# Two groups instead of four for the routing of blocks 6 to 11, with marks made on VectorE, low parts of the first weight pieces on GpSimd, and block 10's row turn inside block 11

## Chip, cores and metric

One core of a Trainium2 chip runs the whole program in one launch. The metric is device time in microseconds. The kernel before ran three times, and the median counts; one more execution was profiled.

## The reference

A linear attention with decay, and behind it a mixture of experts in which each token goes to one expert. What matters of it:

```python
state = gamma * state + einsum('bhd,bhe->bhde', k_t, v_t)      # for each of 768 steps, 4 batches, 8 heads
y_t = scale * einsum('bhd,bhde->bhe', q_t, state)              # head_dim 64
x = y as 3072 rows of 512
xn, en = x / (norm(x) + 1e-6), expert_emb / (norm(expert_emb) + 1e-6)
logits = xn @ en.T / tau                                        # 8 experts
expert_idx, gate = argmax(logits), softmax(logits) at expert_idx
for e in range(8):
    h = relu(x[expert_idx == e] @ w1[e])                        # 512 x 1024
    out[expert_idx == e] = gate * (h @ w2[e])                   # 1024 x 512
```

All in fp32.

## The kernel before, in words

**Blocks.** The 3072 tokens are worked off in 12 blocks of 256 (`for m in range(NM)`, m is 0 to 11). Each block computes scores (L388) that VectorE masks (L408) into `pm`, the part of y from the state (`inter`) and from the block itself (`intra`, both L451), and the state of the next block (L422). TensorE also transposes the next block's keys and queries (L357, L375) in four sets of four. ScalarE copies results out of PSUM (`take`, L467 and L470; L362, L376). VectorE turns the rows of y (L475, `rows_turn`) and SyncE writes them to a table of rows `xd` in HBM (L485, `rows`).

**Banks.** Transpositions, scores, logits and the routing's small products share four PSUM banks in turn (`pt_`, names `b`). A product that takes a bank waits until the bank's reader is done.

**Routing.** Blocks are routed in groups (`GROUPS`). For a group: logits of each block (L498, transposed by VectorE at L506 into `parts`), `sums` (L516), `choose` and `add_counts` (VectorE), `count` (L543 to L547), `ranks`, `split_ranks` (VectorE), `mark`, and `table`. `mark` makes, for each half block of 128 tokens, a 128x128 tile that holds the token's number where its rank stands and 0 elsewhere; ScalarE makes it with two operations (L601, L602). `table` multiplies these by VectorE's columns (L610) and VectorE subtracts the product from `tab` (L615). Six groups stand here: 0 to 2, 3 to 5, 6 and 7, 8, 9 and 10, 11; the marks of the last two are made together.

**Early gather.** In block 10 the table of blocks 0 to 8 is complete. VectorE casts it to `ri` (L668), GpSimd gathers the first 288 rows of expert 0 from `xd` into `xge` (three indirect DMAs, L662), block 9's rows and two weight pieces are loaded or written behind that gather, TensorE turns `xge` (L676) at the end of block 11, and the first layer of expert 0 begins with these rows while blocks 9 to 11 are still being routed.

**Weight pieces.** A piece is 128x1024 of an expert's weights, eight pieces an expert. It is loaded into `raw` (four buffers), ScalarE casts it to `whi` (L227) and VectorE subtracts for the low part `wlo` (L232). Each product of the experts is made of three: high by high, high by low, low by high (L245 in layer 1, L1109 in layer 2 with outputs by column). The four pieces of expert 0's layer 1 are cast in block 10 (`first`) and at its end (`lows`).

**Expert 0's tail.** Generators interleave the first layer (`run(n)` emits n products) with the routing of the last blocks. `hidden` makes the hidden layer's high part on ScalarE (L251) and its low part `hl` on VectorE (L254). The last table stands inside layer 2's first output tile, ahead of its last two steps. From it come the late rows of expert 0 and expert 1's rows: gathered by GpSimd (L662), written and read back by SyncE (L1057, L1080), turned by VectorE (L1090).

The order on each engine is that of the code.

## Time and profile before

| | |
|---|---|
| median of 3 runs | 414.93 us (414.82 to 414.96) |
| profiled execution | 415.67 us, its span 413.9 us |
| TensorE busy | 396.3 us, 96% of the span |
| VectorE, ScalarE, GpSimd busy | 261.4, 234.6, 125.8 us |
| mean granted clock of TensorE | 0.983 |

The span is what the engines' records cover. The profiled execution is one of the program's executions, 0.74 us above the median. Shares of busy time are means over stages that differ, so the stages are looked at one by one.

### The profile page before, as it was taken

The page shows a single profiled execution, that of the slowest core. Times are in us where ns is not written, and L with a number is a line of the kernel's source. Part 1 is how long each engine was busy: PE and PEld are TensorE (multiplying, and loading weights), DVE is VectorE, ACT ScalarE, POOL GpSimd, SP SyncE. Part 2 cuts the span into 40 slices and gives each one's busy share as a digit, 9 for nine tenths or more (in the row PEclk, how much of TensorE's full clock was granted, in tenths as well). Part 3 has the DMA queues.
Part 4 walks back from the last instruction along what each step waited for, and adds up shares of the span by engine and source line. Part 5 has one row for each costly group of instructions (what it writes and reads, how often), then busy time and mean ns, then how long its engine had stood idle before and what let it go on. Part 6 is the DMA issues. An engine that isn't in the chain of part 4 may idle for free.

```text
span 413.9 us, 9654 instructions
## 1 busy us (share of the span) xinstructions
PE 396.3 (96%) x3694; PEld 363.8 (88%) x3694; DVE 261.4 (63%) x587; ACT 234.6 (57%) x438; POOL 125.8 (30%) x141
## 2 busy tenths in 40 slices
PE   6999899999799989999999999999999999999993
PEld 3998788888688988899999999999889989999972
DVE  4497886877669666972775487197276565685500
ACT  3565588598884906743733745375475555563410
POOL 2565653333120042411440360151155052000041
PEclk9999999999889989999999999999999999999998
DMA  8998999799364766969697886889879966934121
GB/s 227 258 291 229 248 253 262 211 254 235 75 155 121 216 203 198 286 205 228 216 300 191 240 283 184 214 290 291 187 272 322 270 207 191 257 130 128 32 96 52
DMA packets 84151, 88.06 MB, mean 213 GB/s; under 512 B 6992, under 2 KB 62800, under 8 KB 84096
## 3 DMA queue, kind: packets, MB, share of 16 engines
q1 hardware_dynamic: 79616, 74.36, 63.5%
q0 software_dynamic: 4304, 12.93, 9.5%
q8 instruction: 31, 0.51, 0.5%
q14 instruction: 24, 0.20, 0.1%
q10 hardware_dynamic: 176, 0.07, 0.1%
HBM read 65.03 MB, written 18.43 MB: 202 GB/s over the span
## 4 chain that ended last, share of the span: by engine, by line
PE 72%; DMA 6%; issue 5%; DVE 5%; SPq 4%; ACT 4%; POOL 2%; POOLq 0%; DVEq 0%; ACTq 0%
PE pst L245 11%; PE b L245 9%; PE py L1109 8%; PE py L245 8%; PE b L1109 6%; PE pst L1109 5%; PE py L451 4%; PE b L1157 4%; PE py L1157 4%; PE b L388 3%; DMA wlo<-in_k_dram 3%; SPq L1121 2%; PE b L357 2%; DMA raw<-in_moe_w_dram 1%; PE b L375 1%
## 5 line engine op out<-in xcount | busy, mean ns | idle before, releaser
L232 DVE TENSOR_TENSOR wlo<-raw,whi 128x1024 fp32r<-128x1024 f32 x64 | 77.8, 1218 | 23.4 <-ACT whi L227 18.1
L1139 POOL DMA_INDIRECT out_dram<-og,si x28 | 29.7, 1060 | 124.9 <-ACT og L1132 83.8
L227 ACT CAST whi<-raw 128x1024 fp32r<-128x1024 f32 x64 | 66.2, 1043 | 0.1
L351 POOL TENSOR_TENSOR hl<-wlo,cst 128x512 f32<-128x512 f32 x22 | 23.0, 1066 | 48.9 <-DVE pm L408 28.4
L662 POOL DMA_INDIRECT xr<-xd,gi x24 | 31.1, 1294 | 16.8 <-DMA raw<-in_moe_w_dram 9.6
L408 DVE TENSOR_TENSOR pm<-b,mask 128x512 f32<-128x512 f32 x48 | 29.8, 682 | 10.0 <-PE b L388 10.0
L1090 DVE STREAM_TRANSPOSE xt<-xg 128x384 f32<-128x384 f32 (+1 forms) x28 | 15.7, 578 | 31.4 <-DMA xg<-xs 31.3
L245 PE MATMUL pst<-xl,whi 128*128 128x380 f32 (+7 forms) x96 | 32.2, 335 | 0.0
L245 PE MATMUL pst<-xh,whi 128*128 128x380 f32 (+7 forms) x96 | 32.0, 334 | 0.0
L245 PE MATMUL pst<-xh,wlo 128*128 128x380 f32 (+7 forms) x96 | 32.0, 333 | 0.0
L245 PE MATMUL b<-xh,whi 128*128 128x408 f32 (+7 forms) x80 | 26.7, 334 | 0.0
L245 PE MATMUL b<-xl,whi 128*128 128x408 f32 (+7 forms) x80 | 26.7, 333 | 0.0
L245 PE MATMUL b<-xh,wlo 128*128 128x408 f32 (+7 forms) x80 | 26.6, 332 | 0.0
L388 PE MATMUL b<-qT,kT 64*128 64x128 f32 x384 | 25.2, 279 | 1.4 <-DVE kT L362 0.9
L245 PE MATMUL py<-xh,whi 128*128 128x288 f32 (+7 forms) x80 | 26.3, 329 | 0.0
L245 PE MATMUL py<-xl,whi 128*128 128x288 f32 (+7 forms) x80 | 26.3, 328 | 0.0
L245 PE MATMUL py<-xh,wlo 128*128 128x288 f32 (+7 forms) x80 | 26.2, 328 | 0.0
L1091 ACT CAST xh<-xt 128x408 fp32r<-128x408 f32 (+6 forms) x28 | 14.2, 510 | 21.0 <-DVE xt L1090 20.7
L388 PEld LDWEIGHTS b<-qT,kT 64*128 64x128 f32 x384 | 22.7, 187 | 2.8 <-ACT kT L362 1.1
L251 ACT ACTIVATE hh<-pst 128x380 fp32r<-128x380 f32 (+7 forms) x24 | 11.6, 482 | 24.0 <-PE pst L245 24.0
L451 PE MATMUL py<-pm,vs 128*64 128x128 f32 x384 | 24.5, 281 | 0.0
L346 POOL TENSOR_TENSOR hh<-whi,cst 128x512 f32<-128x512 f32 x22 | 23.3, 1079 | 0.0
(260 smaller groups left out, 1056.4 us busy)
## 6 DMA issues: line engine op xcount, KB each, us to landing
raw<-in_moe_w_dram SPq DMA_DIRECT2D x60, 512.0 KB, 4.9
whi<-in_q_dram SPq DMA_DIRECT2D x24, 256.0 KB, 4.0
wlo<-in_k_dram SPq DMA_DIRECT2D x11, 512.0 KB, 5.5
xd<-x SPq DMA_DIRECT2D x39, 128.0 KB, 4.2
xs<-xr SPq DMA_DIRECT2D x6, 768.0 KB, 5.0
whi<-in_v_dram SPq DMA_DIRECT2D x6, 512.0 KB, 6.2
wlo<-in_v_dram SPq DMA_DIRECT2D x6, 512.0 KB, 7.4
xg<-xs SPq DMA_DIRECT2D x16, 192.0 KB, 4.4
```

The lines of the kernel that those rows point to most:

```text
L227: nc.scalar.copy(out=hv, in_=rv)
L232: eng.tensor_tensor(out=lv, in0=rv, in1=hv.bitcast(F32), op=ALU.subtract)
L245: nc.tensor.matmul(acc[:, :w], a[:, f], x[:, kt, cols], start=(n == 0), stop=(n == 3 * KT - 1))
L346: return eng.tensor_tensor(out=qs_r[:, m % 3, :, a], in0=qin[m % 3][:, a], in1=w, op=ALU.mult)
L351: return eng.tensor_tensor(out=ks_r[:, m % 3, s, h], in0=kin[m % 3][:, h, s], in1=w[:, h], op=ALU.mult)
L388: nc.tensor.matmul(psc[a][:, j], kTs[m][a * D:(a + 1) * D, j, u].rearrange("p s c -> p (s c)"), q_cols(m, a, j, u), start=True, stop=True, ...
L408: o.append(nc.vector.tensor_tensor(out=pm, in0=psc[a], in1=w, op=ALU.mult))
L451: nc.tensor.matmul(pys[m][u][o * D:(o + 1) * D, j], lhsT, rhs, start=first, stop=True, skip_group_check=True)
L662: return nc.gpsimd.indirect_dma_start(out=xr[:n, j, :], out_offset=None, in_=xd[:rows_, :], in_offset=bass.IndirectOffsetOnAxis(ap=gi[:n, ...
L1109: nc.tensor.matmul(acc[:, :c], a[:, f], x[:, kt, :c], start=(n == 0), stop=(n == 3 * FT - 1))
L1139: i = nc.gpsimd.indirect_dma_start(out=out[:, :], out_offset=bass.IndirectOffsetOnAxis(ap=si[:n, e, j:j + 1], axis=0), in_=og[:n, j, :], i ...
L1157: nc.tensor.matmul(acc[:s, :], x[:, kt, at], a, start=(n == 0), stop=(n == 3 * FT - 1))
```

## The change

Four groups become two: blocks 6 to 8 and 9 to 11. The group of blocks 6 to 8 is summed and chosen in block 9, ranked at block 10's start, marked in block 10, and its table now stands behind the transpositions. The marks of the last two groups are one VectorE operation each. The low parts of the four first pieces go to GpSimd, behind the gathers. Block 10's row turn (`rows(m - 1)`) moves into block 11. In expert 0's tail the marks come behind nine steps of the sort, and the three squares stand 12 products earlier.

```diff
-GROUPS = ((0, 1, 2), (3, 4, 5), (6, 7), (8,), (9, 10), (11,))
+GROUPS = ((0, 1, 2), (3, 4, 5), (6, 7, 8), (9, 10, 11))
...
-    tail = len(GROUPS) - 2
+    tail = len(GROUPS) - 1
...
-        r = span(g) if g < tail else slice(span(g).start, NB)
+        r = span(g)
...
         for i in part:
             n = r.start + i
+            if g >= tail - 1:
+                nc.vector.tensor_scalar(out=hm[i], in0=C("iota"), scalar1=low[:, n:n + 1], scalar2=C("gaps")[:, n:n + 1],
+                                        op0=ALU.is_equal, op1=ALU.mult)
+                continue
             nc.scalar.activation(out=hm[i], in_=C("iota"), func=AF.Square, scale=-1.0, bias=low[:, n:n + 1])
...
-    marks = {4: (0, range(3)), 5: (0, range(3, 6)), 7: (1, range(3)), 8: (1, range(3, 6)), 9: (2, range(4))}
-    tables = {6: 0, 9: 1, 10: 2}
+    marks = {4: (0, range(3)), 5: (0, range(3, 6)), 7: (1, range(3)), 8: (1, range(3, 6))}
+    tables = {6: 0, 9: 1}
...
-            if m == NM - 2:
-                table(waiting)
-                gathered = early_gather()
             if nxt:
                 state_sums(m + 1)
                 spread_v(m, 1, nc.vector.tensor_copy)
...
+                if m == NM - 2:
+                    table(waiting)
+                    gathered = early_gather()
                 rows(m - 1, gathered if m == NM - 2 else None)
                 if m == NM - 2:
                     for f in first:
-                        f()
+                        f(nc.gpsimd)
...
                 intra(m, 0)
-                z = sums(done)
-                run_all(choose(done, z))
-                run_all(add_counts(done))
+                rows(m - 1)
                 for f in lows:
-                    f()
+                    f(nc.gpsimd)
                 intra(m, 1)
-                pr = count(done)
                 ps = [turn_rows(xge, EROWS, kt, bank(f"pst{kt}")) for kt in range(2)]
-                run_all(ranks(done, pr))
...
-    rows(m - 1)
     load_piece()
     load_piece()
     run(11)
...
-    split_ranks(tail)
     first_low()
-    for i in range(6):
-        run(1)
-        mark(tail, (i,))
     for _ in range(9):
         next(sort_steps)
         run(1)
+    split_ranks(g)
+    for i in range(6):
+        run(1)
+        mark(g, (i,))
...
-    run(12)
     for j, n in EROWS:
         square(xge, n, j, j)
+    run(12)
     split()
```

On VectorE in block 10, before, from the columns of block 8's table (`xl`) to the next block's masks (`pm`); `tab` is the table, `ri` its cast, `parts` the transposed logits:

```order
L592 TENSOR_TENSOR xl<-cst_61,col 128x64
L506 STREAM_TRANSPOSE parts<-b_2048 128x256
L615 TENSOR_TENSOR tab<-tab,b_2055 128x32
L615 TENSOR_TENSOR tab<-tab,b_2061 128x32
L668 CAST ri<-tab 128x3
L435 TENSOR_TENSOR s_2075<-pst_1608,tB 128x256
L401 COPY vs<-whi 64x512 x2
L475 STREAM_TRANSPOSE x<-yT 128x4x4x32 x2
L232 TENSOR_TENSOR wlo<-raw,whi 128x1024 x2
L408 TENSOR_TENSOR pm_2164<-b_2154,mask 128x512
```

And now, from the columns of the three blocks' table (`xh`); the six operations from `low` to `xh` are the marks:

```order
L592 TENSOR_TENSOR xh<-cst_61,col 128x192
L602 TENSOR_SCALAR xh<-cst_61,low 128x128 x6
L506 STREAM_TRANSPOSE parts<-b_2013 128x256
L435 TENSOR_TENSOR s_2020<-pst_1608,tB 128x256
L401 COPY vs<-whi 64x512 x2
L619 TENSOR_TENSOR tab<-tab,b_2053 128x32
L672 CAST ri<-tab 128x3
L475 STREAM_TRANSPOSE x<-yT 128x4x4x32 x2
L408 TENSOR_TENSOR pm_2127<-b_2117,mask 128x512
```

The marks stand ahead of the logits' transposition, the table's subtraction has moved behind the spreading of the values (`vs`), and two subtractions of weight pieces are gone.

On TensorE in block 10, before, from the logits (`yT`, `enT`) over the two tables' products to the transpositions:

```order
L498 MATMUL b_2048<-yT,enT 32x256 x4
L610 MATMUL b_2055<-xh 128x32 x4
L610 MATMUL b_2061<-xl 128x32 x2
L357 MATMUL b_2079<-ident,hl 128x128 x4
L375 MATMUL b_2087<-ident,hh 128x128 x4
L375 MATMUL b_2093<-ident,hh 128x128 x4
L357 MATMUL b_2099<-ident,hl 128x128 x4
L621 MATMUL b_2111<-parts,cst_61 32x64
```

And now:

```order
L498 MATMUL b_2013<-yT,enT 32x256 x4
L357 MATMUL b_2024<-ident,hl 128x128 x4
L375 MATMUL b_2032<-ident,hh 128x128 x4
L375 MATMUL b_2038<-ident,hh 128x128 x4
L357 MATMUL b_2044<-ident,hl 128x128 x4
L614 MATMUL b_2053<-xh 128x32 x6
L625 MATMUL b_2074<-parts,cst_61 32x64
```

The table is one, of six products, and stands behind the four sets of transpositions.

On GpSimd from the last scaling of queries to the gather of expert 0's late rows, before:

```order
L346 TENSOR_TENSOR hh<-whi,cst_60 128x8x64 x2
L662 DMA xge<-xd,ri 128x520 x2
L662 DMA xge<-xd,ri 32x520
L968 COPY zs_81<-xge 128x24
L1172 MEMSET xr_2586 128x520
L662 DMA xr_2586<-xd,ri 128x520
```

And now:

```order
L346 TENSOR_TENSOR hh<-whi,cst_60 128x8x64 x2
L666 DMA xge<-xd,ri 128x520 x2
L666 DMA xge<-xd,ri 32x520
L232 TENSOR_TENSOR wlo<-raw,whi 128x1024 x4
L968 COPY zs_81<-xge 128x24
L1171 MEMSET xr_2522 128x520
L666 DMA xr_2522<-xd,ri 128x520
```

Four subtractions of whole pieces stand behind the gathers and ahead of the copy of the gathered scores.

## Rows read from the trace of the kernel before

**Rows 1.** The page's part 1: TensorE's busy time, share and instructions.

```profile
PE 396.3 (96%) x3694; PEld 363.8 (88%) x3694; DVE 261.4 (63%) x587; ACT 234.6 (57%) x438; POOL 125.8 (30%) x141
```

**Rows 2.** Windows: busy us of each engine by stretch, mean granted clock, DMA share.

```profile
91.41:101.42 10.01, 9.66 (x191) 8.53 (x190) 7.39 (x25) 8.03 (x17) 4.05 (x4) 1.00 0.93 243
101.42:117.73 16.31, 12.99 (x166) 11.30 (x164) 11.27 (x33) 13.46 (x26) 3.54 (x3) 0.79 0.50 115
117.73:127.00 9.27, 9.15 (x142) 6.56 (x140) 6.97 (x17) 7.63 (x13) 0.20 (x1) 1.00 0.60 172
127.00:140.82 13.82, 13.82 (x112) 13.32 (x111) 10.70 (x39) 8.76 (x21) 0.00 (x0) 1.00 0.57 154
132.80:147.22 14.42, 12.38 (x88) 11.56 (x87) 10.04 (x28) 11.50 (x27) 0.00 (x0) 1.00 0.77 230
140.82:154.88 14.06, 12.02 (x75) 11.20 (x73) 9.38 (x28) 5.02 (x12) 4.60 (x5) 0.88 0.65 194
171.32:413.90 242.58, 235.84 (x1273) 224.85 (x1271) 137.94 (x279) 120.05 (x208) 65.07 (x62) 0.99 0.70 209
```

**Rows 3.** Timeline, TensorE: start, us, line, operation, count, [idle before <- what ended it].

```profile
96.62 0.84 PE L610 MATMUL b<-xh 128*128 128x32 f32 x6
103.25 1.42 PE L388 MATMUL b<-qT,kT 64*128 64x128 f32 x16 [0.48 <-DVE rs L563]
110.17 0.40 PE L610 MATMUL b<-xl 128*128 128x32 f32 x1 [2.42 <-ACT xl L602]
111.22 1.11 PE L357 MATMUL b<-ident,hl 128*128 128x128 f32 x4
```

**Rows 4.** Timeline, ScalarE, block 10: the casts of two weight pieces.

```profile
107.31 1.98 ACT L227 CAST whi<-raw 128x1024 fp32r<-128x1024 f32 x2
```

**Rows 5.** Windows of 1 us in block 10 (the clock is PEclk).

```profile
110.00:111.00 1.00, 0.41 (x2) 0.30 (x2) 0.00 (x0) 0.90 (x3) 0.00 (x0) 0.50 0.00 0
116.00:117.00 1.00, 1.00 (x18) 1.00 (x16) 0.59 (x1) 0.88 (x4) 0.26 (x1) 0.72 0.56 200
```

**Rows 6.** Timeline, TensorE: gathered rows turned; layer 2 of expert 0.

```profile
123.92 1.13 PE L676 MATMUL pst<-ident,xge 128*128 128x128 f32 x6
147.00 0.40 PE L1109 MATMUL pst<-hl,whi 128*128 128x288 f32 x1 [0.93 <-DVE hl L254]
148.14 0.44 PE L1109 MATMUL pst<-hh,whi 128*128 128x288 f32 x1
```

**Rows 7.** Timeline, VectorE, block 10: the four masks, the logits' transposition.

```profile
104.15 2.48 DVE L408 TENSOR_TENSOR pm<-b,mask 128x512 f32<-128x512 f32 x4
107.33 0.44 DVE L506 STREAM_TRANSPOSE parts<-b 128x256 f32<-128x256 f32 x1
```

**Rows 8.** VectorE's costs: a group by form; L401's min/median/max in ns.

```profile
L592 DVE TENSOR_TENSOR xh<-cst,col 128x128 fp32r<-128x128 f32 x1 | 0.3, 293 | 0.0
L401 DVE COPY vs<-wlo x10: 422/425/1270, 24.4 to 98.8; 64x512 f32<-64x512 f32 x10
```

**Rows 9.** GpSimd: timeline, then line L346's min/median/max in ns.

```profile
94.14 2.05 POOL L351 TENSOR_TENSOR hl<-wlo,cst 128x512 f32<-128x512 f32 x2 [5.27 <-DVE pm L408]
112.11 1.27 POOL L662 DMA_INDIRECT xge<-xd,ri  x1 [13.93 <-DVE ri L668]
115.00 1.26 POOL L662 DMA_INDIRECT xge<-xd,ri  x1 [0.30 <-issue]
118.28 0.20 POOL L968 COPY zs<-xge 128x24 f32<-128x24 f32 x1 [2.02 <-DMA xge<-xd,ri]
L346 POOL TENSOR_TENSOR hh<-whi,cst x22: 1037/1043/1491, 13.5 to 97.1; 128x512 f32<-128x512 f32 x22
```

**Rows 10.** Expert 1's reads: issues, landing after issue; VectorE's timeline behind them.

```profile
L1080 SPq DMA_DIRECT2D xg<-xs x4: 329/473/842, 161.0 to 162.8; - x4
DMA to landing us min/median/max: 2.9/4.7/5.3
168.66 1.10 DVE L1090 STREAM_TRANSPOSE xt<-xg 128x416 f32<-128x416 f32 x2
```

More of the change, by code (lines that the diff above doesn't have):

```diff
@@ L583, in split_ranks @@
         if g < tail:
-            t = hp.tile([P, 8, P], F32R, name="xl" if g == tail - 1 else "xh")
+            t = hp.tile([P, 8, P], F32R, name="xh")
             hm = [t[:, i] for i in range(6)]
```

## Prediction

> **What bounds the kernel now.** I read the page first: TensorE is busy for 96% of the span [rows 1], so only a stretch in which it is not, or in which its clock is low, can give much. I then cut the span at block starts and at expert 0's layers [rows 2]. Block 9 takes 10.01 us with 9.66 busy. Block 10 takes 16.31 us with 12.99 busy at a mean granted clock of 0.79. Expert 0's first layer (127.00 to 140.82) has no gap. The stretch behind it, 140.82 to 154.88, has 12.02 busy of 14.06 at 0.88. All that follows, 171.32 to the end, is 97% busy (235.84 of 242.58). The reader should see that the two poor stretches are the ones that the change touches.
>
> Block 10's timeline shows why [rows 3]. TensorE reaches the table's last two products and waits 2.42 us for the mark of block 8 (`xl`, L602). ScalarE makes those marks only behind the casts of two weight pieces, which start at 107.31 and take 1.98 us [rows 4]. [...]
>
> The second poor stretch is layer 2 of expert 0. Its last products of the first output tile wait for VectorE's low part of the hidden layer until 147.00 [rows 6]; VectorE itself worked 10.04 of the 14.42 us between its first such part and the table (132.80 to 147.22), because ScalarE had marks, casts and squares in turn ahead of what VectorE needed [rows 2].
>
> **The change, step by step** (times of the profiled execution: 415.67 us, 413.9 of it the span; the median of the runs is 0.74 less, and I carry the difference over unchanged).
>
> *Block 9.* Sums, choice and counts of blocks 6 and 7 leave its front, where TensorE lost 0.35 us (10.01 less 9.66). ScalarE's marks for the table of blocks 3 to 5 stay and are now what TensorE meets next, so I take 0.3 sooner.
>
> *Block 10.* With the marks gone from ScalarE, nothing holds the table as before. Its products become those of block 9 (that block has a table too, more state products and a shorter count, which I let cancel): 9.66 us. A new wait appears. VectorE now does six marks ahead of the transposition (L506) that hands back a PSUM bank, and TensorE's fourth set of transpositions needs that bank. The masks end at 106.6 now [rows 7], about 1.0 sooner then (0.35, TensorE's 0.48 at the second scores [rows 3], and the split of the four-block group no longer ahead of them): 105.6. Then the split, about 0.9 (0.7 now, from the masks' end to L506 at 107.33, with fewer columns); six marks; and 0.44 for L506. A mark has no row. Nearest above is the 128x128 product at 0.293, which makes 1.8 us for six; below, a copy of 512 columns takes 0.42, a quarter of it 0.11 and six 0.6 [rows 8]. I take 0.21 each (the row of that size less the overlap of neighbours), 1.3 in all, so the bank is free at 108.3. TensorE's three earlier sets end near 107.4: the wait that ends at 110.17 began at 107.75, behind four table products (0.6), so the logits end at about 106.1 when all is 1.0 sooner, and three sets at full clock take some 0.45 each (half of the 1.11 at 111.22, less overlap). The wait is 0.9; the bounds make it 0.2 to 1.4. That is below the 2.42 in which the clock fell, and other waits, such as the 0.48, did not move it, so I keep the full clock. Block 10: 16.31 less (9.66 + 0.9), **5.75 saved**.
>
> *Gather.* The table now stands behind the transpositions: 108.3, 0.55 for the last set, 0.7 for the table (its 0.84 in block 9 less overlap [rows 3]), 0.7 for subtraction, cast and GpSimd's start give 110.3, against 112.11 [rows 9], 1.8 sooner. The rows land 1.8 sooner than the 118.28 at which the copy that waits for them starts: 116.5. TensorE wants them at 123.92 less 6.0 less 0.35, about 117.6. Hidden, with 1.1 to spare.
>
> *Block 11.* Sums and count of blocks 9 and 10 leave it; they stand for about 0.5 of its 9.27 us. Block 10's row turn moves ahead of block 11's second half; its four DMAs keep their place on SyncE's queue, behind block 9's rows and two loads, and those follow the gather. ScalarE's small copy for it waits for one TensorE product in the same block. I price this at nothing; its cover is the 1.1 us above. **0.5 saved.** First layer at 120.5 instead of 127.0.
>
> *Low parts on GpSimd.* Four subtractions of 128x1024 stand behind the three gathers on GpSimd, and the copy of the gathered scores waits behind them, which nothing needs soon. Two 128x512 products take 2.05 there [rows 9], so I take 2.05 a piece. The third gather's issue ends at 116.26 less 1.8, near 114.5; with a start of 0.3 the four end at 116.8, 118.9, 120.9 and 123.0. The first layer's twelfth product wants the fourth at 122.2: **0.75 lost**. The dearest 128x512 product took 1.49, so a piece may be 2.98 and the loss 4.5; at the price that VectorE pays for a piece nothing is lost.
>
> *Expert 0's tail.* VectorE gets the six marks of the last group (1.3 us and the split) and loses nothing else, but its 4.38 us of waiting go almost wholly, since ScalarE no longer makes marks there and the squares stand one tile earlier. Starting 6.5 sooner (126.3), with 10.04 + 1.3 and some 0.7 of waits, it reaches the table at 138.3, 8.9 sooner. TensorE then finds each part half a microsecond before it needs it. The first output tile takes 24 products and the table: 24 x 0.133 + 0.75 = 3.95 instead of 7.32 (140.82 to 148.14 [rows 6]): **3.4 saved**. The next 42 products took 6.74 (148.14 to 154.88), in part at half clock; at 0.133 they are 5.6: **1.1 saved**.
>
> *Expert 1's rows.* They hang on VectorE's table, 8.9 sooner, while TensorE would be 0.3 + 5.75 + 0.5 - 0.75 + 3.4 + 1.1 = 10.3 sooner. The last of the four reads lands at most 5.3 and at least 2.9 us behind its issue at about 162.8, and VectorE turns them at 168.66 [rows 10]: 0.6 to 3.0 us of slack. 1.4 less that leaves 0 to 0.8 given back; I take **0.8**, since VectorE is packed there.
>
> **Sum:** 10.3 - 0.8 = 9.5. Profiled 406.2, span 404.4, median 414.93 - 9.5 = **405.4**. Behind 171.32 the loads are paced by the pieces' release, so the whole rest shifts.
>
> **Rivals.**
> 1. *The clock falls anyway*, in block 10 or at the wait for the fourth low part. For it: it fell in the wait of 2.42, and it is 0.88 on the mean in the broken stretch behind 140.82. Price: TensorE at half speed from 111.22 to 116 and at 0.72 for one more is 2.7 us of work lost. 405.4 + 2.7 = 408.1. Chance 0.13.
> 2. *GpSimd and VectorE hold each other.* A VectorE copy of 0.42 took 1.27 once, and a GpSimd product of 1.04 took 1.49 [rows 8, 9]. At 2.98 a piece the loss is 4.5 instead of 0.75: 409.1. Against it: most of VectorE's work in that time, masks and the rows' low parts, reads one operand from PSUM (the masks' row names a bank, `b` [rows 7]). Chance 0.11. [...]
> 3. *The front's gain stops at expert 1*: the gathers for it don't come sooner, because something other than the table holds them, and TensorE waits at 171. Then 414.9. Against it: block 11's rows are written long before those gathers. Chance 0.05.
> 4. *Slower*: the fourth low part at a piece price from about 4.45 us, since four such pieces less the 7.45 between 114.75 and 122.2 eat the 10.25 won elsewhere. At 5 us a piece: 414.93 - 10.25 + 20 - 7.45 = 417.2. Against it: none of the 22 products of that line went past 1.49 for half a piece. Chance 0.04.
>
> **How the numbers follow.** My forecast has 0.62 (403.9 to 407.5), rivals 1 to 4 have 0.13, 0.11, 0.05 and 0.04; 0.05 is left for less than 403.9 (no wait for low parts, none given back). The range reaches to rivals 1 and 2: 403.9 to 409.6. A measurement of this kernel can tell about 0.2% from no change, 0.8 us. Faster 0.91, same 0.05, slower 0.04.
>
> **What would show it.** Right: no wait of 2 us at block 10's table and the clock at 1.00 there; a wait of about 1 us ahead of the fourth transposition set, put down to VectorE's L506; gathers issued near 110; first layer from about 120.5; low parts of 2.05 on GpSimd and a wait below 1 us for the fourth; no waits in layer 2's first tile; expert 1 from about 161.8. Wrong: marks above 0.3 us, low parts above 2.3 us, a clock of 0.50 anywhere before 150, or TensorE idle for expert 1's rows by more than 1 us.

## The result, and the profile after

| | before | after |
|---|---|---|
| median | 414.88 us (414.57 to 414.96, 4 runs) | 405.61 us (404.6 to 406.26, 4 runs) |
| profiled execution, its span | 415.67, 413.9 us | 405.7, 403.9 us |
| mean granted clock of TensorE | 0.983 | 0.998 |

The ratio is 0.9776, 95% interval 0.9755 to 0.9797: faster by 9.3 us. 405.4 was predicted.

Of the page's part 1 after, the line that answers to [rows 1]: TensorE is busy 5.5 us less (four transpositions of L357 took 1.11 us [rows 3] at a clock of 0.50 and take 0.66 at 1.00), ScalarE 9.8 and VectorE 3.0 less, GpSimd 11.2 more.

```profile
PE 390.8 (97%) x3676; PEld 359.6 (89%) x3676; DVE 258.4 (64%) x571; ACT 224.8 (56%) x414; POOL 137.0 (34%) x145
```

The windows of the kernel after, by about the same stretches as [rows 2] (block 9, block 10, block 11, layer 1 of expert 0, layer 2 up to the late rows). Their edges don't stand at quite the same products (block 9's stretch begins 0.71 us ahead of its scores before and 0.19 behind them now), so they show clock and gaps, and what a stage gained is taken from starts further below:

```profile
91.20:101.00 9.80, 9.80 (x196) 8.68 (x196) 6.82 (x19) 8.37 (x18) 4.05 (x4) 1.00 1.01 256
101.00:111.70 10.70, 9.81 (x166) 8.68 (x166) 9.56 (x30) 8.34 (x15) 1.39 (x2) 1.00 0.55 121
111.70:120.50 8.80, 8.80 (x130) 6.41 (x127) 5.68 (x12) 7.45 (x14) 8.47 (x5) 1.00 0.52 128
120.50:134.90 14.40, 13.13 (x112) 12.73 (x111) 11.79 (x40) 8.28 (x17) 2.85 (x3) 1.00 0.85 259
134.90:144.50 9.60, 9.60 (x74) 9.50 (x74) 8.19 (x27) 0.80 (x3) 3.49 (x4) 1.00 0.63 199
```

The reader is to see two things. The clock is 1.00 in every one, where block 10 had 0.79 and layer 2 had 0.88. And TensorE has gaps in two of them only (10.70 less 9.81, 14.40 less 13.13), of 0.89 and 1.27 us. Its timeline names them (the rows answer to [rows 3, 6]):

```profile
108.04 0.66 PE L357 MATMUL b<-ident,hl 128*128 128x128 f32 x4 [0.89 <-DVE parts L506]
111.33 2.06 PE L388 MATMUL b<-qT,kT 64*128 64x128 f32 x32
117.20 1.15 PE L680 MATMUL pst<-ident,xge 128*128 128x128 f32 x6
119.93 0.40 PE L245 MATMUL py<-xh,whi 128*128 128x288 f32 x1
123.26 0.40 PE L245 MATMUL py<-xh,wlo 128*128 128x288 f32 x1 [1.27 <-POOL wlo L232]
135.00 0.30 PE L1108 MATMUL pst<-hh,whi 128*128 128x288 f32 x1
144.62 0.60 PE L1183 MATMUL b<-ident,xr 128*128 128x128 f32 x4
162.76 0.45 PE L245 MATMUL pst<-xl,whi 128*128 128x408 f32 x1 [0.24 <-DVE xl L1096]
```

The wait for the mark (2.42 us) is gone, the one foreseen for VectorE's transposition stands in its place, the gathered rows are turned at 117.20 without a wait, and layer 2 has none either. VectorE's timeline, with the marks of block 10 and of the tail (answers to [rows 7]), and GpSimd's with its low parts (answers to [rows 9]), the last row being the minimum, median and maximum of those in ns:

```profile
106.00 1.63 DVE L602 TENSOR_SCALAR xh<-cst,low 128x128 fp32r<-128x128 f32 x6
107.54 0.44 DVE L506 STREAM_TRANSPOSE parts<-b 128x256 f32<-128x256 f32 x1
122.43 0.85 DVE L531 SCALAR_TENSOR_TENSOR w<-w,cst 128x48 f32<-128x48 f32 x1
131.69 1.63 DVE L602 TENSOR_SCALAR pm<-cst,low 128x128 fp32r<-128x128 f32 x6
138.47 0.18 DVE L619 TENSOR_TENSOR tab<-tab,b 128x32 f32<-128x32 f32 x1
110.01 1.27 POOL L666 DMA_INDIRECT xge<-xd,ri  x1 [12.93 <-DVE ri L672]
113.86 9.35 POOL L232 TENSOR_TENSOR wlo<-raw,whi 128x1024 fp32r<-128x1024 f32 x4
L232 POOL TENSOR_TENSOR wlo<-raw,whi x4: 2354/2377/2401, 113.9 to 120.9; 128x1024 fp32r<-128x1024 f32 x4
```

### The profile page after: what moved, and what is told of

The parts are those of the page before. It is cut to its first block, busy times and chain, and to the rows that moved or that the text cites. A ratio compares the mean times of both kernels' runs of the same rounds, so it can differ in the third digit from the quotient of the medians.

```text
span 403.9 us, 9580 instructions
## 1 busy us (share of the span) xinstructions
PE 390.8 (97%) x3676; PEld 359.6 (89%) x3676; DVE 258.4 (64%) x571; ACT 224.8 (56%) x414; POOL 137.0 (34%) x145
## 4 chain that ended last, share of the span: by engine, by line
PE 68%; DVE 11%; DMA 8%; issue 6%; SPq 4%; POOL 2%; ACT 0%; POOLq 0%; DVEq 0%
PE pst L245 10%; PE b L245 8%; PE py L1108 7%; PE py L245 7%; PE py L451 6%; PE b L1108 5%; PE pst L1108 4%; PE b L1156 4%; PE py L1156 4%; PE b L388 4%; SPq L1120 2%; DMA xd<-x 2%; PE pst L422 2%; PE b L357 2%; DVE pm L408 2%
## 5 line engine op out<-in xcount | busy, mean ns | idle before, releaser
L232 DVE TENSOR_TENSOR wlo<-raw,whi 128x1024 fp32r<-128x1024 f32 x60 | 73.1, 1219 | 16.9 <-ACT whi L227 13.0
L666 POOL DMA_INDIRECT xr<-xd,gi x24 | 32.1, 1337 | 14.9 <-ACT sq L286 7.7
L245 PE MATMUL pst<-xl,whi 128*128 128x380 f32 (+7 forms) x96 | 32.2, 335 | 0.2 <-DVE xl L1096 0.2
L245 PE MATMUL pst<-xh,whi 128*128 128x380 f32 (+7 forms) x96 | 32.1, 334 | 0.0
L245 PE MATMUL pst<-xh,wlo 128*128 128x380 f32 (+7 forms) x96 | 32.0, 333 | 0.0
L245 PE MATMUL py<-xh,wlo 128*128 128x288 f32 (+7 forms) x80 | 26.2, 328 | 1.3 <-POOL wlo L232 1.3
L245 PE MATMUL b<-xh,whi 128*128 128x408 f32 (+7 forms) x80 | 26.7, 334 | 0.0
L245 PE MATMUL b<-xl,whi 128*128 128x408 f32 (+7 forms) x80 | 26.7, 333 | 0.0
L245 PE MATMUL b<-xh,wlo 128*128 128x408 f32 (+7 forms) x80 | 26.6, 332 | 0.0
L245 PE MATMUL py<-xh,whi 128*128 128x288 f32 (+7 forms) x80 | 26.3, 329 | 0.0
L245 PE MATMUL py<-xl,whi 128*128 128x288 f32 (+7 forms) x80 | 26.2, 327 | 0.0
L388 PE MATMUL b<-qT,kT 64*128 64x128 f32 x384 | 25.0, 279 | 0.9 <-DVE kT L362 0.9
L388 PEld LDWEIGHTS b<-qT,kT 64*128 64x128 f32 x384 | 22.7, 187 | 2.3 <-ACT kT L362 1.1
L271 POOL TENSOR_TENSOR r<-r,half 128x4 f32<-128x4 f32 (+1 forms) x9 | 8.9, 994 | 43.2 <-DVE r L270 43.2
```

Of the source, the lines that this page charges most:

```text
L232: eng.tensor_tensor(out=lv, in0=rv, in1=hv.bitcast(F32), op=ALU.subtract)
L245: nc.tensor.matmul(acc[:, :w], a[:, f], x[:, kt, cols], start=(n == 0), stop=(n == 3 * KT - 1))
L388: nc.tensor.matmul(psc[a][:, j], kTs[m][a * D:(a + 1) * D, j, u].rearrange("p s c -> p (s c)"), q_cols(m, a, j, u), start=True, stop=True, ...
L666: return nc.gpsimd.indirect_dma_start(out=xr[:n, j, :], out_offset=None, in_=xd[:rows_, :], in_offset=bass.IndirectOffsetOnAxis(ap=gi[:n, ...
```

## The experiments

The kernel before read 414.88 us in the first set of runs and 416.53, 415.06 and 415.05 in the three sets below, so each kernel is held against the kernel before of its own set. The runs of one kernel spread by 1.3 to 5.6 us there, more than some edits are worth, and of these three sets only the last holds the changed kernel itself (e0, beside e6, e7 and e11). So the traces are compared too, by a ruler that leaves the start out: block 9's scores (L388) begin at 90.45 to 94.97 us in the fourteen profiles, 94.97 being e9's, an execution that was late from its first block on (its granted clock was 0.50 there, from 11 to 14 us, where after's was 1.00). The table counts from there to the first product (L388) of block 11, of expert 0's layers 1 and 2 (L245; L1109, which is L1108, L1104 or L1113 in other versions), to layer 2's first product into a bank `b`, and to that of expert 1's layer 1. All are differences of start times on TensorE's timeline: before, 117.73 less 92.12 is 25.61. Behind the last of these points every profile has 239.9 to 240.0 us left (before 413.9 less 92.12 less 81.81; after 403.9 less 91.01 less 72.92), so all of the kernels differ ahead of it alone.

| kernel | median, us | ratio to before (95%) | block 11 | layer 1 | layer 2 | its `b` | expert 1's `b` |
|---|---|---|---|---|---|---|---|
| before | | 1 | 25.61 | 34.88 | 48.70 | 60.36 | 81.81 |
| after | 405.61 | 0.9776 (0.9755 to 0.9797) | 20.32 | 28.92 | 43.99 | 51.21 | 72.92 |
| e0, after again | 406.12 | 0.9809 (0.9761 to 0.9857) | 20.32 | 28.93 | 43.99 | 51.20 | 74.19 |
| e3, marks on ScalarE | 416.75 | 1.0042 (1.0015 to 1.007) | 24.57 | 33.37 | 47.09 | 61.34 | 82.87 |
| e6, last marks on ScalarE | 412.86 | 0.9944 (0.9922 to 0.9965) | 20.31 | 28.92 | 43.98 | 59.31 | 80.75 |
| e4, before, marks on VectorE | 407.77 | 0.9809 (0.9764 to 0.9854) | 21.04 | 30.31 | 44.14 | 51.47 | 74.64 |
| e5, before, filled wait | 412.48 | 0.9928 (0.9905 to 0.9952) | 23.03 | 32.29 | 46.12 | 57.76 | 79.20 |
| e10, before, casts behind | 412.37 | 0.9948 (0.992 to 0.9976) | 21.51 | 31.33 | 45.16 | 58.04 | 79.48 |
| e7, squares late | 406.82 | 0.9789 (0.9757 to 0.9821) | 20.33 | 28.93 | 43.97 | 51.18 | 74.08 |
| e1, low parts on VectorE | 405.82 | 0.9736 (0.971 to 0.9761) | 20.33 | 29.08 | 42.81 | 50.50 | 73.02 |
| e2, low parts split | 407.10 | 0.9782 (0.9757 to 0.9806) | 20.32 | 29.64 | 43.79 | 51.00 | 73.11 |
| e8, marks behind | 405.63 | 0.9734 (0.9709 to 0.9759) | 19.48 | 29.40 | 43.99 | 51.20 | 73.99 |
| e9, e8 and e2 | 407.82 | 0.9776 (0.9746 to 0.9805) | 19.34 | 29.28 | 43.69 | 50.90 | 73.37 |
| e11, e8 and e1 | 405.57 | 0.9776 (0.974 to 0.9811) | 19.33 | 28.94 | 42.67 | 50.52 | 72.27 |

Theory at the start: the gain is that ScalarE no longer makes marks, in block 10 (a wait and the clock that falls in it) and in expert 0's tail; the other parts shift waits about. Rival: the joined groups, the table's place and the squares make it.

**e0: the changed kernel again,** in the set of e6, e7 and e11, with no edit.

> The changed kernel itself, as the yardstick of the three runs beside it, since the kernel before read 414.9 us on the first chip, 416.5 on the second and 415.1 on the third. Expected: 405 to 407 us, ratio 0.974 to 0.978.

Measured: 406.12 us, from 405.12 to 410.7. Up to layer 2 its profile repeats the first one to 0.01 us; only expert 1's `b` comes 1.27 us later, for a reason met again under e11.

**e3: the marks' engine undone.** All marks on ScalarE, the rest of the change kept.

```diff
-            if g >= tail - 1:
-                nc.vector.tensor_scalar(out=hm[i], in0=C("iota"), scalar1=low[:, n:n + 1], scalar2=C("gaps")[:, n:n + 1],
-                                        op0=ALU.is_equal, op1=ALU.mult)
-                continue
```

> The changed kernel with all marks made by ScalarE again, two operations each; the two groups, the low parts on GpSimd, the table behind the transpositions and block 11's order stay. Theory (the marks' engine is what the gain hangs on): twelve operations of some 0.43 us stand on ScalarE ahead of the copies of the transpositions, so the table's columns and then the copies of keys come about 4 us later, TensorE waits 2 us or more once or twice in block 10, the clock falls to 0.5 for some us as before, and in expert 0's tail VectorE waits for ScalarE again: 409 to 412 us. Rival (the order of the groups and of the table does it): 406.5 us or less, clock 1.00 throughout block 10.

Measured: 416.75 us, slower than the kernel before by 0.15 to 0.7%, and 4.75 us above the dearest figure expected. ScalarE's and TensorE's timelines in block 10, and the window of 1 us after the wait:

```profile
105.76 0.40 ACT L601 ACTIVATE xh<-cst,low 128x128 fp32r<-128x128 f32 x1 [0.65 <-DVE col L581]
110.69 0.56 ACT L362 COPY kT<-b 128x512 f32<-128x512 f32 x1
111.31 0.84 PE L610 MATMUL b<-xh 128*128 128x32 f32 x6 [3.66 <-ACT kT L362]
113.00:114.00 1.00, 1.00 (x13) 1.00 (x11) 0.92 (x2) 0.96 (x3) 1.00 (x1) 0.50 0.06 16
```

Twelve operations fill ScalarE from 105.76 to the copy of keys at 110.69, 0.82 us a mark. TensorE waits 3.66 us for that copy, and the clock falls to 0.50 behind the wait. Block 11 begins 4.25 us later than after, which is what was expected of the whole; the tail then takes 14.25 us from layer 2 to its `b` instead of 7.22, 7.0 more, which I had put far too low. Without the marks on VectorE the rest of the change is a loss.

**e6: the last group's marks alone on ScalarE.**

```diff
-            if g >= tail - 1:
+            if g == tail - 1:
```

> The changed kernel with the marks of its last group alone (blocks 9 to 11, in expert 0's tail) on ScalarE, two operations each; block 10's stay on VectorE. Theory (ScalarE's row is what held expert 0's tail, so twelve operations there bring back more than the eight of the kernel before): block 10 is as in the changed kernel, the low parts and casts of the tail come late, waits of 2 us or more together and a clock of 0.5 for some us behind the first output tile: 5 to 7 us more than the changed kernel. Rival (the tail was held by VectorE's own work or by the squares, and the marks are hidden): at most 1.5 us more, clock 1.00.

Measured: 412.86 us, 6.74 above e0 beside it; the theory holds. Up to layer 2 nothing moves (43.98); its `b` comes 8.1 us later. ScalarE's timeline there, TensorE's, and the windows of layer 2's first stretches:

```profile
132.68 0.40 ACT L605 ACTIVATE pm<-cst,low 128x128 fp32r<-128x128 f32 x1 [3.73 <-DVE low L579]
137.62 0.39 ACT L251 ACTIVATE hh<-pst 128x288 fp32r<-128x288 f32 x1
138.99 0.40 PE L1108 MATMUL pst<-hh,whi 128*128 128x288 f32 x1 [1.69 <-ACT whi L227]
140.25 0.40 PE L1108 MATMUL pst<-hh,wlo 128*128 128x288 f32 x1 [0.73 <-DVE wlo L232]
136.34:144.93 8.59, 5.87 (x26) 4.58 (x25) 5.00 (x7) 7.67 (x18) 0.00 (x0) 0.75 0.39 108
144.93:154.00 9.07, 9.07 (x49) 9.04 (x50) 4.90 (x23) 0.00 (x0) 5.40 (x6) 0.68 0.56 162
```

The reader is to see the chain: the marks hold the hidden layer's casts back (from 132.68 to 137.62), TensorE then waits for a piece's cast, and the work behind it runs at a mean clock of 0.75 and 0.68.

**e4: the marks alone.** The kernel before, with the marks of its last four groups on VectorE.

```diff
+            if g >= 2:
+                nc.vector.tensor_scalar(out=hm[i], in0=C("iota"), scalar1=low[:, n:n + 1], scalar2=C("gaps")[:, n:n + 1],
+                                        op0=ALU.is_equal, op1=ALU.mult)
+                continue
```

> The kernel before with one edit: the marks of its last four groups (blocks 6 and 7, 8, 9 to 11) are made by VectorE in one operation each. Theory (marks on VectorE alone free block 10): TensorE's wait of 2.42 us at the table of block 8 falls below 0.5, the clock stays at 1.00, block 10 comes down from 16.3 to 11 or less, and expert 0's layer 2 loses part of its waits: 6 to 8 us less than before. Rival (the joined groups and the moved table are needed): less than 4 us.

Measured: 407.77 us, 7.3 less than before: the theory holds. TensorE's timeline in block 10 and in layer 2:

```profile
104.26 1.42 PE L388 MATMUL b<-qT,kT 64*128 64x128 f32 x16 [1.50 <-DVE rs L563]
108.83 0.45 PE L614 MATMUL b<-xl 128*128 128x32 f32 x2
139.01 0.38 PE L614 MATMUL b<-pm 128*128 128x32 f32 x2
```

Both tables find their marks ready, though VectorE's extra work makes the 0.48 us at the second scores [rows 3] 1.50, and block 10 takes 11.55 us, a little more than the 11 expected. Block 11 begins 4.57 us sooner than before; the whole change has 5.29. At layer 2 the two are 0.15 us apart, and layer 2's first stretch takes 7.33 us where the whole change takes 7.22.

**e5: the clock's price alone.** The kernel before with products of constants in the wait.

```diff
+            if m == NM - 2:
+                fill = bank("pst1")
+                for _ in range(34):
+                    nc.tensor.matmul(fill[:, :P], ones, tri, start=True, stop=True)
```

> The kernel before with 34 extra products of constants into a free bank ahead of the last table of block 10: TensorE is busy during the wait of 2.42 us, and the marks come when they came. The output is unchanged; the work is added. Theory (the clock falls because TensorE stood still, and the lost 2.7 us of block 10 are the clock's price, not the wait's): the clock stays near 1.00 through 110 to 117, the wait for the mark is still there in full as filler, and the time is 2 to 2.7 us less than before. Rival (the clock falls for another reason, or the filler only takes the place of the wait): within 0.8 us of before or slower, with 0.5 in that stretch.

Measured: 412.48 us, 2.58 less than before, and block 11 begins 2.58 us sooner too. TensorE's timeline (L912 is the filler) and the two windows that stood at 0.50 and 0.72 in [rows 5]:

```profile
107.04 2.07 PE L912 MATMUL pst<-tri,ones 128*128 128x128 f16 x34
109.60 0.28 PE L610 MATMUL b<-xl 128*128 128x32 f32 x1 [0.49 <-ACT xl L602]
110.42 0.28 PE L610 MATMUL b<-xl 128*128 128x32 f32 x1 [0.54 <-ACT xl L602]
110.00:111.00 1.00, 0.58 (x5) 0.58 (x6) 0.23 (x2) 0.37 (x1) 0.00 (x0) 1.00 0.00 0
116.00:117.00 1.00, 1.00 (x28) 0.88 (x28) 1.00 (x2) 0.97 (x2) 0.00 (x0) 1.00 0.28 79
```

The mark that is waited for comes no sooner (its product starts 18.05 us behind block 9's scores in both), yet the clock stays at full speed. Block 10 alone, from its scores to block 11's, in before and in after:

```profile
101.61:117.73 16.12, 12.80 (x163) 11.13 (x160) 11.08 (x33) 13.39 (x26) 3.54 (x3) 0.79 0.49 114
100.76:111.33 10.57, 9.69 (x164) 8.55 (x161) 9.80 (x31) 8.34 (x14) 1.27 (x1) 1.00 0.58 127
```

So of the 5.55 us that block 10 gains (16.12 less 10.57), some 2.6 is the clock's, which fell because TensorE stood still, and 2.44 is idle time that is gone (3.32 less 0.88). The half microsecond that is left was not taken apart.

**e10: the casts' place.** The kernel before, with the two casts behind block 10's marks.

```diff
-        if m == NM - 2:
-            first = [split_cast(), split_cast()]
...
             mark(waiting, range(2 * len(GROUPS[waiting])))
+            first = [split_cast(), split_cast()]
```

> The kernel before with the two casts of weight pieces put behind block 10's marks on ScalarE instead of ahead of them. Theory (what holds the marks back is the 1.98 us of casts in ScalarE's row, so the wait of 2.42 is theirs): the wait shrinks to 0.4 to 0.8 us, the clock stays at 1.00 and the time is 4 to 5 us less than before; marks on VectorE are then worth less in block 10 than the casts' place. Rival (the marks wait for VectorE's ranks, or the casts then hold the copies of the keys just as long): the wait moves to the copies behind the casts, 1.5 us or more, and less than 2 us are won.

Measured: 412.37 us, 2.69 less than before, between the two. In block 10 the theory holds: the waits shrink to 0.52 and 0.54 us, the clock is 1.00 and block 11 begins 4.10 us sooner. In the tail TensorE's waits are those of before (0.44 us for VectorE's `wlo`, 0.68 for ScalarE's `hh`, 0.93 for VectorE's `hl`), the clock falls behind them as it did before, to a mean of 0.67 in the 5 us from 140, and stays low for longer, so the tail takes 12.88 us to its `b` instead of 11.66. Why it stays low for longer was not taken apart. TensorE's waits in block 10 and the two windows:

```profile
107.18 0.28 PE L610 MATMUL b<-xl 128*128 128x32 f32 x1 [0.52 <-ACT xl L602]
108.00 0.28 PE L610 MATMUL b<-xl 128*128 128x32 f32 x1 [0.54 <-ACT xl L602]
106.00:112.00 6.00, 4.63 (x53) 4.07 (x50) 4.42 (x12) 5.93 (x12) 1.90 (x2) 1.00 0.33 72
140.00:145.00 5.00, 3.40 (x16) 3.09 (x16) 3.56 (x11) 1.27 (x3) 0.53 (x1) 0.67 0.70 259
```

So block 10 alone could have been mended by order on ScalarE. The tail is not mended by this reorder; another order in the tail itself was not tried.

**e7: the squares' place undone.**

```diff
+    run(12)
     for j, n in EROWS:
         square(xge, n, j, j)
-    run(12)
     split()
```

> The changed kernel with the three squares of expert 0's rows put back behind 12 more products. Theory (with the marks off ScalarE the squares cost the tail little): 2.46 us of squares then stand ahead of the next output tile's casts; layer 2 waits 0 to 0.6 us and the time is within 0.8 us of the changed kernel's. Rival (the squares' place is a good part of the tail's 3.4 us): 1 to 2.5 us more, with waits for the hidden layer's high parts or for a weight piece's cast in layer 2's first tile.

Measured: 406.82 us, 0.7 above e0 with both spread by 3 us or more. The profile shows no wait in layer 2, and 7.21 us to its `b`. The squares' place is worth nothing once the marks are off ScalarE.

**e1, e2: where the low parts are made.** e1 makes all four on VectorE (both hunks), e2 the last two (the second hunk alone).

```diff
                     for f in first:
-                        f(nc.gpsimd)
+                        f()
...
                 for f in lows:
-                    f(nc.gpsimd)
+                    f()
```

> All four low parts go back to VectorE; the rest is the changed kernel (405.6 us). Theory (the move to GpSimd costs the 1.27 us that TensorE waits for the fourth low part, and spares VectorE 2.2 us ahead of block 11's masks and 2.2 ahead of the xge low parts): the wait of 1.27 goes, but VectorE's first two subtractions stand behind the row turn that ends near 111.0 and push the masks from 112.5 to about 113.2, which holds TensorE some 0.7 us; the sum is 0.4 to 0.8 us faster than the changed kernel, 404.8 to 405.2. Rival (the move gives part of the gain, VectorE is too packed): 406.5 us or more, with waits of TensorE for masks and for the low parts of xge of 2 us together.

> The first two low parts stay on GpSimd, the last two go to VectorE, which waits for ScalarE from 116.7 to 118.9 in the changed kernel. Theory (TensorE's wait of 1.27 us is the fourth piece's place in GpSimd's queue and nothing else): GpSimd's two end near 118.6, VectorE's two take 1.1 each in the idle stretch, the wait goes and the time is 1.0 to 1.3 us less, 404.3 to 404.6. Rival (VectorE's subtraction has both operands in SBUF and is held while GpSimd reads there, as the choice of the last group seems to be, 0.85 instead of 0.21): VectorE's pieces show 1.5 us or more while GpSimd works on its own, the low parts of xge come about 1 us later, and the time is within 0.3 us of the changed kernel's.

Measured: e1 405.82 us, e2 407.10. e2's rival holds in what it says of VectorE's pieces. GpSimd's and VectorE's lines in e2 (the second row the minimum, median and maximum), and TensorE's in block 11:

```profile
114.12 4.70 POOL L232 TENSOR_TENSOR wlo<-raw,whi 128x1024 fp32r<-128x1024 f32 x2
L232 DVE TENSOR_TENSOR wlo<-raw,whi x2: 1217/1602/1986, 117.9 to 119.8; 128x1024 fp32r<-128x1024 f32 x2
118.77 1.20 POOL L968 COPY zs<-xge 128x24 f32<-128x24 f32 x1
114.70 0.71 PE L451 MATMUL py<-qT,s 64*64 64x128 f32 x16 [0.27 <-issue]
```

VectorE's first piece begins at 117.9 while GpSimd is on its second until 118.82 (114.12 and 4.70), and takes 1.99 us; the next takes 1.22. The expected 1.5 us or more shows, but it is the smaller part of what eats the gain: it costs TensorE some 0.3 us in layer 1, whose second product waits for VectorE's `xl`. Layer 1 itself begins 0.72 us later than after, and the cause stands ahead of VectorE's pieces: block 11's products of the state (`py<-qT,s`) take 1.74 us instead of 1.03, around a gap put down to "issue", and are over at 115.3, ahead of 117.9. So the wait of 1.27 us goes, and layer 2 begins only 0.20 us sooner. By the table e2 ends within 0.2 us of the first profile after, as its rival has it; by its median it is 1.0 us above e0, which was run in another set.

In e1 GpSimd is free and the wait of 1.27 us goes. VectorE's masks begin at 113.28, as expected, and hold TensorE by less than expected: block 11 takes 8.75 us instead of 8.60. Layer 2 begins 1.18 us sooner, so the move of the low parts to GpSimd costs that much up to there. Expert 1's `b` stands at 73.02, 0.10 us behind the first profile after and 1.17 ahead of e0's. By the medians neither of e1's expectations is met; by the ratios e1 and e8 would be some 0.4% below the changed kernel, with intervals that overlap, and the changed kernel was not run beside them. So their times don't tell them from it.

**e8, e9: the marks behind the logits' transposition,** alone and with e2's edit.

```diff
             split_ranks(waiting)
-            mark(waiting, range(2 * len(GROUPS[waiting])))
...
                 logits_rows(i, logits_products(i))
+            if m == NM - 2:
+                mark(waiting, range(2 * len(GROUPS[waiting])))
```

> Block 10's six marks stand behind the logits' transposition on VectorE instead of ahead of it; the rest is the changed kernel. Both expect the wait of 0.89 us ahead of the fourth set of transpositions to go. Theory (from there to the fourth low part GpSimd's chain sets the end: table, three gathers, four pieces): the table's columns are ready no earlier, so the gathers and the pieces stay where they are, the wait for the fourth piece grows from 1.27 to about 2.1 us and the time is within 0.3 us of the changed kernel's. Rival (the two waits are independent): 0.9 us less, 404.7.

> The marks behind the logits' transposition and the last two low parts on VectorE, together. Theory (both waits hang on one chain, GpSimd's): with the chain shortened the 0.9 us of the first wait now reaches the first layer, and the sum is larger than that of the two edits alone: 1.8 to 2.2 us less than the changed kernel, 403.4 to 403.8. Rival (additive, or the gather becomes the bound: TensorE would want the gathered rows at 116.3 and the marks behind the transposition leave the gathers near 110): 1.0 us less, 404.6, with a wait of about 1 us ahead of the turn of the gathered rows.

Measured: e8 405.63 us, e9 407.82. In both the wait of 0.89 us goes and block 11 begins 0.84 and 0.98 us sooner. In e8 the fourth low part is waited for until 122.72, which is 32.27 us behind block 9's scores, and 32.25 after (123.26 less 91.01): GpSimd's chain ends where it did, as the theory has it. The wait did not grow to 2.1, because block 11 itself became 1.32 us longer (9.92 instead of 8.60); 0.81 and 1.32 make the 2.1. TensorE's timeline in e8:

```profile
113.13 0.44 PE L451 MATMUL py<-qT,s 64*64 64x128 f32 x4 [0.24 <-issue]
122.72 0.40 PE L245 MATMUL py<-xh,wlo 128*128 128x288 f32 x1 [0.81 <-POOL wlo L232]
```

Gaps put down to "issue", for which the profile shows nothing that was waited for, also stand among block 11's products of the state in e2 (0.27 us) and e9 (twice 0.29), and in none of after, e0, e1, e6, e7 and e11. These products take 1.03 us after, 1.74 in e2, 2.34 in e8 and 2.37 in e9, so the gaps are all that block 11 lost in these three. What they are stays open. e9's sum of 1.8 to 2.2 us did not come: of the 0.98 won ahead of block 11 and the 1.27 behind it, 1.34 went into block 11 and some 0.6 into a longer wait for VectorE's `xl`, and layer 2 begins 0.3 us sooner. So neither its theory nor its rival is decided; its profile has no wait at the turn of the gathered rows, so the rival's bound is not seen. The profiled execution of e9 is its dearest (410.04), late by 4 us from the start; of its other five there is no trace.

**e11: both waits of the front removed** (e8's and e1's edits together).

> The changed kernel with all four low parts on VectorE and block 10's marks behind the logits' transposition: both waits of TensorE's front (1.27 and 0.89 us) should go. Theory (what the front wins is given back ahead of expert 1's first layer, whose rows are read back no earlier than about 158.5 whenever their reads are issued): layer 2 starts 1.5 us sooner or more, the waits for expert 1's rows grow by as much, and the time is within 0.5 us of the changed kernel's beside it. Rival (the front's gain passes through): 1.5 to 2.0 us less than the changed kernel, which would then be the better version.

Measured: 405.57 us (403.63 to 407.37) against e0's 406.12 (405.12 to 410.7): 0.55 us less at the median, and not to be told apart. Both waits go, but layer 2 begins 1.32 us sooner instead of 1.5 or more. TensorE's timeline in block 11 shows why:

```profile
113.94 0.64 PE L498 MATMUL b<-yT,enT 128*32 128x256 f32 x8 [0.38 <-DVE pm L408]
116.08 0.30 PE L625 MATMUL b<-parts,cst 128*32 128x64 f32 x2 [0.46 <-DVE parts L506]
```

VectorE, which has the low parts back, is now late with the masks and the transposition, 0.84 us together. In layer 2's first stretch 0.63 more is given back (7.85 us to its `b` instead of 7.22), where VectorE works 7.32 of the 7.85. What becomes of the rest hangs on the reads of expert 1's rows. VectorE's timeline in e0, where it waits for them, and in e11:

```profile
159.61 1.11 DVE L1089 STREAM_TRANSPOSE xt<-xg 128x416 f32<-128x416 f32 x2 [1.45 <-DMA xg<-xs]
158.13 1.11 DVE L1090 STREAM_TRANSPOSE xt<-xg 128x416 f32<-128x416 f32 x2 [0.21 <-DMA xg<-xs]
```

and the reads in after and in e11 (starts of the first and last, then landing after issue):

```profile
L1079 SPq DMA_DIRECT2D xg<-xs x4: 329/474/1094, 152.7 to 154.8; - x4
DMA to landing us min/median/max: 2.8/3.5/3.5
```

```profile
L1080 SPq DMA_DIRECT2D xg<-xs x4: 328/474/1191, 151.6 to 153.7; - x4
DMA to landing us min/median/max: 3.7/4.3/4.6
```

The first read is issued at 152.7, and in e11 at 151.6; the four land 0.8 us more slowly there by the median, and VectorE turns the rows at 158.7 and 158.1. Over after, e0, e1, e2, e8 and e11 that turn begins between 158.1 and 159.6 us, with reads issued between 151.6 and 152.7. e0's 1.45 us of waiting against after's 0.18, with the same code, shows how much differs from one execution to the next. The waits did not grow in e11, as the theory had it: its own is 0.21 us, and its expert 1 has its `b` at 72.27, 0.65 us ahead of the first profile after and 1.92 ahead of e0's. So neither the theory nor the rival is shown, and no better version is claimed. Why the reads land as they do was not taken apart.

Read over all rows, the table says more. From layer 2's `b` to expert 1's it is 21.4 to 21.5 us in the five kernels whose tail has its marks on ScalarE (before, e3, e5, e6, e10), and 21.7 to 23.2 in the nine whose tail has them on VectorE. So 0.3 to 1.7 us of what the faster tail wins is lost again ahead of expert 1, and the first profile after (21.71) lost least.

## Why the prediction was right

The forecast of 405.4 us held (405.61), by its own mechanism; the profiled execution gained 10.0 us. By its steps, with starts from TensorE's timelines:

- **Block 9**, 0.3 foreseen, and **block 10**, 5.75. From block 8's scores to block 9's it is now 8.54 us instead of 9.32, so 0.78; from there to block 10's 9.75 instead of 9.49, so 0.26 lost; from there to block 11's 10.57 instead of 16.12, so 5.55 (the last two together are the table's 5.29). The sum of 6.07 is the forecast's 6.05. Block 10 takes what was put (9.66 and 0.9); its 16.31 had 0.19 of block 9's end in it. For block 9 only the 0.35 us of waiting was counted and not the products that leave its front, nor that block 9 itself gets 0.26 us longer. Block 10's new wait is 0.89 us for L506, 0.9 foreseen; marks take 0.27 us each instead of 0.21. The clock kept 1.00, and e5 confirms the 2.7 us at which rival 1 priced it (2.58).
- **Gather** at 110.01, 110.3 foreseen, and hidden, as foreseen.
- **Block 11**: 0.67 (9.27 less 8.60), 0.5 foreseen; first layer at 119.93, 120.5 foreseen.
- **Low parts**: the mis-sized term. 2.05 us a piece was taken from two products of half the size [rows 9], a row of another shape; 2.38 was measured (the row of 2377 ns), above the 2.3 that the prediction named as a sign against it. The wait is 1.27 us instead of 0.75, and layer 1 lost 1.25 (15.07 less 13.82). It would have been longer had the pieces not begun 0.9 us sooner than put (113.86 against 114.75): the four took 9.35 us instead of 8.2. Rival 2 is not what did it: in e2 VectorE's piece takes 1.99 us instead of 1.22, GpSimd's take 2.35 again (half of 4.70). What the prediction set against this rival is borne out: the masks, the last of them from 114.3 us on beside GpSimd's first piece, take 0.68 us each after as before, and the rows' low parts beside its third 0.45 each, as before without any.
- **Tail**: layer 2 up to the late rows' turn takes 9.62 us (144.62 less 135.00) instead of 14.06, 4.4 saved, 3.4 and 1.1 foreseen; the table's subtraction is at 138.47, 138.3 foreseen. e6 and e4 show that it is the marks' engine; e7 shows that the squares' place, which the prediction named as a second reason, is worth nothing beside it. Whether it would be worth something with the marks on ScalarE was not tried.
- **Expert 1's rows**: 0.26 us given back in the profiled execution (0.24 of it the wait at 162.76), 0.8 foreseen, but 1.27 more in e0. Rival 3 thus exists in small: 0.3 to 1.7 us are lost there in the nine profiles with the marks on VectorE, and the 0.8 put lies inside. Whether a sooner layer 2 gets through is not shown: e1 and e11 win 1.2 to 1.3 us there and keep -0.10 and 0.65 against after, 1.17 and 1.92 against e0.
- What is left of the 10.0 us is 0.33 us by which the profiled execution was ahead at block 8's scores already (82.47 against 82.80), which no step of the change explains.

Net: 0.33 + 0.78 + 5.29 + 0.67 - 1.25 + 4.44 - 0.26 = 10.0. The low parts' loss, larger by 0.5, and the smaller loss at expert 1 cancelled; that the total is this close is in part luck. Marks on VectorE alone (e4) make 7.3 of some 9 us; the other parts of the change together add the rest, 1.65 or 2.16 us by the medians of e0 and after. Of it 0.78 us lies ahead of block 9's scores (e4 takes the 9.32 of before there), 0.15 stands at layer 2, and what is left lies at expert 1's rows, where two executions of the same code were 1.27 us apart. No run undoes the joined groups or the table's place alone, so their shares stay open. The low parts on GpSimd are no gain up to layer 2: e1, without them, is there 1.18 us sooner.

## What to carry to other kernels

When an engine that feeds the bound one is late, ask whether the work is in the wrong order or on the wrong engine: a reorder mended block 10 (e10) but not the tail, where ScalarE worked without a pause from 134.14 to 145.90 us in the kernel before. Price a stall of TensorE with the granted clock that was measured behind it: here some 2.6 us on top of the wait of 2.42, shown by filling that wait with useless products, while behind the waits of 0.89 and 1.27 us after the clock stayed at 1.00. And a wait that is removed need not show in the time: two waits of 1.27 and 0.89 us went in e11, VectorE's fuller row gave 0.84 and 0.63 us back, and what is left is less than two executions of the same code differ by at a chain of transfers behind it.

## What was not expected of the hardware

- A VectorE subtraction with both operands in SBUF took longer beside one on GpSimd: 1.99 us instead of 1.22 in e2, the excess being about what GpSimd had left (0.9 us); in e9, with 1.4 left, 2.46. The choice's L531 takes 0.85 us after, ending with GpSimd's last piece, and 0.21 in e1, where GpSimd has no pieces. The other way too: GpSimd's small copy behind its pieces starts in e2 while VectorE's first piece runs, ends with it, and takes 1.20 us (1.22 in e9) instead of 0.20 after. In these rows it is the one that began second that took longer; GpSimd's own pieces, which began first, show no loss (2.35 us in e2, 2.38 after).
- A GpSimd subtraction of 128x1024 with two whole operands takes 2.38 us, while two of 128x512 took 2.05 [rows 9].
- The clock fell to 0.50 at a wait of TensorE of 2.4 us before (it was 0.50 from 110 to 116 us) and of 3.7 us in e3, and stayed at 1.00 through 0.89 and 1.27 us after, two waits of some 0.5 us in e5 and in e10's block 10, and 1.50 us in e4. It also fell without a single long wait: in the tail of before TensorE waited 0.44, 0.68 and 0.93 us between 143 and 147 us, and the clock was 0.50 from 148 to 150.
